# Retention and two expert layers: decay powers by scans, early loads, constants in pieces, noisy logits in two parts

## The chip, the cores and the metric

The program runs on one core of a Trainium2 chip. The metric is the device time of one execution in microseconds (us). The engines are named as the profile names them: PE is TensorE's matmul, PEld its weight load, DVE is VectorE, ACT is ScalarE, POOL is GpSimd, SP is the engine whose queue issues most transfers. An engine takes its instructions in the order in which they stand in its queue; a wait in one holds all behind it.

## What is computed

Two batches of 768 tokens with 8 heads of 64 go through a retention layer, and the 1536 rows of 512 that come out go through two expert layers of 8 experts (512 to 1024 to 512). The part that matters here is the first:

```python
Dmask = np.where(rel >= 0, lam[:, None, None] ** rel[None, :, :], 0.0)
intra = np.einsum('bhic,bhjc->bhij', qb, kb) * Dmask[None]
intra = np.einsum('bhij,bhjd->bhid', intra, vb)
inter = np.einsum('bhid,bhde->bhie', qb * lam_pow[None], kv_state)
out[:, :, sl] = intra + inter
kv_state = lam_block[None, :, None, None] * kv_state + np.einsum('bhsd,bhse->bhde', kb * rev_pow, vb)
```

The second layer's input is chosen by noisy logits: `logits + log1p(exp(x @ w_noise)) * noise`. The two largest of a token name its experts.

## The kernel before, in words

Retention is computed in blocks of 128 tokens instead of the reference's 64, so there are twelve tiles j, six to a batch. For each tile the loop at lines 772 to 819 issues, in this order: the loads of tile j + 2 (`load`, line 152: k, v and, for every second tile, q of two tiles); `scores(j)` (line 610: 16 products of k and q, then the two VectorE products "at" with the decay matrix `dm`); `rows(j - 1)` (line 665: the tile before is turned into rows, its logits are summed on VectorE, its rows are stored to `x1` by SP); `front(j + 1)` (line 604: k and q of the next tile are turned on TensorE; GpSimd makes `kd`, k times the decay factors `dk`, and the four `qd`, q times its powers `pq`); conversions of expert weights (`convert` on ScalarE and `convert_low` on VectorE, lines 101 and 112); `mix(j)` (line 645: the product of `qd` and the state, L651, then of "at" and v, L657, the ScalarE copy `xT`) and, within it, `state(j)` (line 623: the product of `kd` and v, L631, the VectorE sum, and the GpSimd multiply of the state by `dec`, L643); last, loads of expert weights (`fetch`, line 84).

A planner orders each engine's queue by the program's order and by when it expects an instruction to be ready. The author corrects it by hand: `with tc.issue_after(x)` puts each instruction of the block that runs on x's engine behind x in its queue, without a wait, and `behind("name")` does so for the instruction last noted in `turn` under that name.

Before the loop, the powers of lam are made. VectorE doubles a row of powers on 8 partitions (line 187), ScalarE's queue writes it to DRAM (line 189), and two loads read it back as `dm`, each partition a shifted window (line 193). The load of v of tile 0 waits for VectorE (line 190), and k of tile 1 and all after it stand behind the loads of `dm` (line 195). A transpose gives `dk` (line 203), and seven products on 128 partitions give `pq` and `dec` (lines 208 to 216).

Other work is woven into the twelve tiles. GpSimd makes the constants of the expert layers at j = 2 in one run behind `kd` of tile 1 (line 780, `more_constants`). The first expert job takes 288 of the first nine tiles' tokens: the noisy logits of tiles 0 to 5 (`noisy` and `first_marked`, line 811) are made at j = 7, their ranks and one-hot marks at j = 8 (line 806); tiles 6 to 8 follow at j = 9 and 10, and the rows are gathered from `x1` at j = 10 (line 792). Eight parts of the first expert's weights are loaded and converted on the way; the experts then run one after the other, each on 128 to 408 rows, in three products of split numbers (line 842).

Of the kernel before, what the change touches and what calls it, by code (L numbers as in the profile page):

```python
# [8 lines left out]
F32 = mybir.dt.float32  # L9
# [11 lines left out]
P = 128  # L21
# [16 lines left out]
def kernel(ctx: ExitStack, tc: tile.TileContext, q, k, v, lam, g1, gn, noise,  # L38
# [24 lines left out]
    powers = dram.tile([1, H, 2 * P], F32, name="powers")  # L63
# [68 lines left out]
    def wait_for(i, other):  # L132
        tc.add_manual_dep(i.ins, other.ins.name, mybir.DependencyInfo(
            mybir.DependencyClass.Sync, mybir.DependencyReason.DATA), reason="a transfer behind other work")

# [43 lines left out]
    pw = rt.tile([P, 2, ROW], F32, name="xg", bufs=4).rearrange("p a b -> p (a b)")[:H, :2 * P]  # L179
    nc.vector.memset(pw[:, P - 1:P], 1.0)  # L180
    nc.vector.memset(pw[:, P:], 0.0)
    nc.vector.tensor_copy(pw[:, P - 2:P - 1], lamh[:H])
    m = 1
# [17 lines left out]
    dk = consts.tile([P, H, 1], F32, name="dk")  # L201
    ps = bank("yp3", [P, H])
    nc.tensor.transpose(ps, pw[:, :P], ident[:H, :H])
    decays = nc.vector.tensor_copy(dk[:, :, 0], ps).ins
    pq = aw.tile([P, HP, P], F32, name="pq", bufs=1)
    dec = consts.tile([P, HP, 1], F32, name="dec")
# [50 lines left out]
    def more_constants():  # L257
        nc.gpsimd.memset(tri, 1.0)
        nc.gpsimd.affine_select(out=tri, in_=tri, compare_op=OP.is_gt, fill=0.0, base=0,
                                pattern=[[1, P]], channel_multiplier=-1)  # L260
        nc.gpsimd.memset(ones, 1.0)
        iota(slot1, [[1, SLOTS]], 1, 0)
        iota(e_up, [[1, E]], 0, 0)
        iota(e_dn, [[-1, E]], E, 0)
        iota(e_row, [[TS, E]], 0, 0)
        iota(trash, [[P, NT]], TABR, 1)
        iota(tok_t, [[P, NT]], 0, 0)
        iota(tok_p, [[0, 1]], 0, 1)
        iota(steps_p, [[P, 5]], 0, 0)
        past_sizes(past1, FIRST, 4)  # L270
        past_sizes(past2, SECOND, 3)
        for c in range(2):
            nc.gpsimd.tensor_copy(who[:, :, c, 0], tok_p.to_broadcast([P, NT]))
            nc.gpsimd.tensor_scalar(who[:, :, c, 1], tok_t, 1.0 / P, 1.0 + 16 * c, op0=OP.mult, op1=OP.add)
        for a in (aux1, aux2):
            nc.gpsimd.tensor_copy(a[:, :, 0], tok_p.to_broadcast([P, NT]))
            nc.gpsimd.tensor_copy(a[:, :, 1], tok_t)
            nc.gpsimd.memset(a[:, :, 2], 1.0)
        nc.gpsimd.memset(mb1, 0.0)
        nc.gpsimd.memset(mbA, 0.0)  # L280
        nc.gpsimd.memset(mb2, 0.0)
        nc.gpsimd.memset(ent1, 0)
        nc.gpsimd.memset(ent2, 0)
        for c in range(2):
            nc.gpsimd.iota(ent2[:, :, c:c + 1], pattern=[[P, NT], [0, 1]], base=0, channel_multiplier=1)
            nc.gpsimd.iota(ent1[:, :, c, 0:1], pattern=[[P, NT], [0, 1]], base=0, channel_multiplier=1)
            nc.gpsimd.iota(ent1[:, :, c, 1:2], pattern=[[2 * P, NT], [0, 1]], base=c, channel_multiplier=2)
# [296 lines left out]
    def front_k(j):  # L584
# [988 lines left out]
```

## Time and profile before

| | |
|---|---|
| Median of 3 runs | 613.4 us (612.31 to 613.89) |
| Profiled execution | 613.06 us, its span 611.5 us |
| Mean granted TensorE clock | 0.991 |
| PE busy | 588.7 us |
| PEld busy | 555.9 us |
| DVE busy | 373.6 us |
| ACT busy | 279.5 us |
| POOL busy | 183.7 us |

The profile is of one execution. Its span goes from the first to the last instruction, and what is missing to the execution's time lies around it. Busy times are shares of the whole; a stretch has to be looked at by itself to see what limits it. In the timeline, "x8" means eight instructions merged into one line, and the bracket at its end is the idle time before it and what ended that.

### The profile page before, as it was taken

What the parts mean: (1) busy time and instruction counts of PE and PEld (TensorE: products, weight loads), DVE (VectorE), ACT (ScalarE), POOL (GpSimd) and SP (SyncE); (2) the same over time, 40 slices, a digit from 0 to 9 for tenths busy, and PEclk for the clock granted to TensorE, in tenths of its full rate; (3) what the DMA queues carried; (4) which work ended last, traced back from release to release, by engine and by line L of the source; (5) the groups of instructions that cost most, each with busy time, mean ns of one, the idle gap of its engine ahead of it and who ended that gap; (6) DMA issues with size and microseconds to landing.
All of it is one profiled execution on the core that took longest, in us unless ns stands there. A gap on an engine that the chain in (4) does not pass through costs nothing. (4 is left out here: it accounts for less than half of the span.)

```text
span 611.5 us, 11514 instructions
## 1 busy us (share of the span) xinstructions
PE 588.7 (96%) x4261; PEld 555.9 (91%) x4261; DVE 373.6 (61%) x861; ACT 279.5 (46%) x488; POOL 183.7 (30%) x254
## 2 busy tenths in 40 slices
PE   6898899999999999999999999999999999999996
PEld 4787788999999999999999999998889999998995
DVE  4375878967445454363554655465896666666993
ACT  3366442145443353353443534127136466467782
POOL 4953440152405005031050230123165525331203
PEclk9999899999999999999999999999999999999998
DMA  7999620554826437546464440273189967966840
GB/s 173 234 266 237 185 69 31 184 158 144 318 97 217 146 109 259 153 158 209 135 212 138 152 161 1 60 273 114 35 260 346 348 222 226 347 195 201 272 143 34
DMA packets 106081, 110.35 MB, mean 180 GB/s; under 512 B 35895, under 2 KB 81983, under 8 KB 106016
## 3 DMA queue, kind: packets, MB, share of 16 engines
q1 hardware_dynamic: 97936, 83.57, 45.0%
q0 software_dynamic: 8064, 25.95, 12.1%
q8 instruction: 35, 0.57, 0.4%
q14 instruction: 30, 0.25, 0.1%
q10 hardware_dynamic: 16, 0.01, 0.0%
HBM read 92.48 MB, written 18.79 MB: 182 GB/s over the span
## 5 line engine op out<-in xcount | busy, mean ns | idle before, releaser
L115 DVE TENSOR_TENSOR wl<-wst,wh 128x1024 fp32r<-128x1024 f32 x107 | 134.7, 1268 | 53.6 <-ACT wh L109 53.4
L109 ACT CAST wh<-wst 128x1024 fp32r<-128x1024 f32 x107 | 111.1, 1048 | 32.5 <-PE yp L844 25.5
L843 PE MATMUL hp<-x,wh 128*128 128x372 f32 (+9 forms) x352 | 116.5, 331 | 0.8 <-ACTq L1400 0.4
L844 PE MATMUL hp<-x,wh 128*128 128x372 f32 (+9 forms) x352 | 116.0, 330 | 0.0
L845 PE MATMUL hp<-x,wl 128*128 128x372 f32 (+9 forms) x352 | 115.2, 328 | 0.0
L927 ACT ACTIVATE h<-hp 128x372 fp32r<-128x372 f32 (+9 forms) x88 | 41.3, 469 | 156.2 <-PE hp L845 143.1
L843 PE MATMUL yp<-h,wh 128*128 128x372 f32 (+8 forms) x320 | 106.8, 334 | 0.0
L845 PE MATMUL yp<-h,wl 128*128 128x372 f32 (+8 forms) x320 | 106.3, 332 | 0.0
L844 PE MATMUL yp<-h,wh 128*128 128x372 f32 (+8 forms) x320 | 105.5, 330 | 0.0
L928 DVE SCALAR_TENSOR_TENSOR h<-hp,h 128x372 fp32r<-128x372 f32 (+9 forms) x88 | 46.4, 527 | 61.8 <-ACT h L927 61.6
L1050 POOL DMA_INDIRECT x<-y,Rdst x25 | 24.7, 989 | 177.9 <-DVE y L1021 175.9
L843 PEld LDWEIGHTS hp<-x,wh 128*128 128x128 f32 x352 | 66.1, 188 | 2.1 <-ACTq L1400 0.7
L844 PEld LDWEIGHTS hp<-x,wh 128*128 128x128 f32 x352 | 66.2, 188 | 0.5 <-DVE x L1200 0.2
L845 PEld LDWEIGHTS hp<-x,wl 128*128 128x128 f32 x352 | 66.2, 188 | 0.1
L844 PEld LDWEIGHTS yp<-h,wh 128*128 128x128 f32 x320 | 60.3, 188 | 0.3 <-DVE h L928 0.2
L845 PEld LDWEIGHTS yp<-h,wl 128*128 128x128 f32 x320 | 60.3, 188 | 0.2 <-issue 0.2
L843 PEld LDWEIGHTS yp<-h,wh 128*128 128x128 f32 x320 | 60.1, 188 | 0.0
L835 DVE TENSOR_TENSOR x<-tr,x 128x128 fp32r<-128x128 f32 (+11 forms) x68 | 27.4, 435 | 27.5 <-ACT x L834 27.0
L834 ACT CAST x<-tr 128x128 fp32r<-128x128 f32 (+11 forms) x68 | 24.5, 386 | 32.8 <-PE tr L833 32.1
L540 POOL TENSOR_TENSOR xg<-xg 128x512 f32<-128x512 f32 (+1 forms) x16 | 26.3, 1647 | 41.7 <-DMA xg<-x,Tsrc 26.6
L529 POOL DMA_INDIRECT xg<-x,Rsrc x25 | 29.5, 1179 | 18.9 <-DVE slt L499 11.6
L1012 PE MATMUL tr<-iw,yT 128*128 128x136 f32 (+2 forms) x224 | 34.2, 287 | 0.1
(386 smaller groups left out, 1029.2 us busy)
## 6 DMA issues: line engine op xcount, KB each, us to landing
wst<-in_moe_w_dram SPq DMA_DIRECT2D x107, 512.0 KB, 4.9
more<-in_moe_w_dram SPq DMA_DIRECT2D x21, 512.0 KB, 5.6
ldk<-in_k_dram SPq DMA_DIRECT2D x12, 256.0 KB, 5.2
ldv<-in_v_dram SPq DMA_DIRECT2D x12, 256.0 KB, 4.4
x<-xr SPq DMA_DIRECT2D x12, 256.0 KB, 2.8
out_dram<-zero SPq DMA_DIRECT2D x12, 256.0 KB, 5.0
ldq<-in_q_dram SPq DMA_DIRECT2D x5, 512.0 KB, 7.6
ldq<-in_q_dram SPq DMA_DIRECT2D x2, 256.0 KB, 3.7
```

The lines of the kernel that those rows point to most:

```text
L109: tail["cast"] = nc.scalar.copy(hi, st).ins
L115: tail["low"] = nc.vector.tensor_sub(lo, st, hi.bitcast(F32)).ins
L529: i = nc.gpsimd.indirect_dma_start(out=r, out_offset=None, in_=x, in_offset=bass.IndirectOffsetOnAxis(ap=src(s)[:m], axis=0))
L540: tail["both"] = nc.gpsimd.tensor_add(a, a, b).ins
L835: v_ = nc.vector.tensor_sub(lo[:, d, :n], ps[:, :n], hi[:, d, :n].bitcast(F32))
L843: nc.tensor.matmul(ps, a[0], b[0], start=start, stop=False)
L844: nc.tensor.matmul(ps, a[0], b[1], start=False, stop=False)
L845: tail["pe"] = nc.tensor.matmul(ps, a[1], b[0], start=False, stop=stop).ins
L927: tail["act"] = nc.scalar.activation(hh, ps, AF.Relu).ins
L928: tail["dve"] = nc.vector.scalar_tensor_tensor(hl, ps, 0.0, hh.bitcast(F32), op0=OP.max, op1=OP.subtract).ins
L1012: nc.tensor.matmul(ps[:m, i, :], self.yT[:, 2 * b + i, s * r:s * r + m], iw[:, 2 * b + i, gates2], start=True, stop=True)
L1050: i = nc.gpsimd.indirect_dma_start(out=target, out_offset=bass.IndirectOffsetOnAxis(ap=dst, axis=0), in_=y, in_offset=None, bounds_check=t ...
```

## The change

- The row of powers, its store to DRAM and the loads of `dm` go. VectorE makes each head's 128 x 128 decay matrix by a scan along its columns (`dm[:, h, i] = lam * dm[:, h, i - 1] + ident[:, i]`), eight scans. `dk` is the last column of that matrix.
- The powers of q are made by four scans instead of seven products; `dec` is their last column.
- lam is loaded first, to all partitions; v of tile 0 and k, v of tile 1 and q of tile 2 follow without a wait, the gate loads behind them.
- Six products of zeros, which nothing reads, are put ahead of the first transposes on TensorE, and two more between those of k and of q.
- The constants are made in five pieces at j = 0 to 4, each behind the GpSimd multiply of the state.
- Conversions: one at each of j = 2 to 5, instead of one, two, two at j = 3, 4, 5.
- `noisy` is cut in two. For tiles 0 to 5 the first half stands ahead of the scores of j = 7, the rest (`noisy_end`) behind its "at". Ranks and marks stand right behind the scores of j = 8.

```diff
-    lamh = consts.tile([P, 1], F32, name="lamh")
     lamb = consts.tile([P, H], F32, name="lamb")
-    nc.sync.dma_start(lamh[:H], bass.AP(tensor=lam.tensor, offset=lam.offset, ap=[[1, H], [1, 1]]))
+    nc.sync.dma_start(lamb, bass.AP(tensor=lam.tensor, offset=lam.offset, ap=[[0, P], [1, H]]))
     rows_of("k", k, 0)
     load_q(0)
-    nc.sync.dma_start(lamb, bass.AP(tensor=lam.tensor, offset=lam.offset, ap=[[0, P], [1, H]]))
+    written = rows_of("v", v, 0).ins
...
-    while m < P:
-        n = min(m, P - 1 - m)
-        a = P - 1 - m
-        last = nc.vector.tensor_scalar(pw[:, a - n:a], pw[:, P - 1 - n:P - 1], pw[:, a:a + 1], None, op0=OP.mult)
-        m *= 2
-    nc.scalar.dma_start(powers.rearrange("o h m -> (o h) m"), pw)
-    wait_for(rows_of("v", v, 0), last)
-    dm = [aw.tile([P, HP, P], F32, name=f"dm{s}", bufs=1) for s in range(2)]
-    for s in range(2):
-        written = nc.sync.dma_start(dm[s], bass.AP(tensor=powers.tensor, offset=powers.offset + s * 2 * P,
-                                                   ap=[[1, P], [4 * P, HP], [1, P]])).ins
+    def unread(n):
+        ps = bank("yp1", [P, P])
+        for _ in range(n):
+            turn["front"] = nc.tensor.matmul(ps, zero, zero, start=True, stop=True).ins
+
+    turn = {}
+    unread(6)
+
+    dm = aw.tile([P, H, P], F32, name="dm", bufs=1)
+    dk = dm[:, :, P - 1:]
+    for h in range(H):
+        decays = nc.vector.tensor_tensor_scan(dm[:, h, :], lamb[:, h:h + 1].to_broadcast([P, P]), ident, 0.0,
+                                              OP.mult, OP.add).ins
     with tc.issue_after(written):
         rows_of("k", k, 1)
+        rows_of("v", v, 1)
+        load_q(2)
         nc.sync.dma_start(iw[:, :, :E], g1.rearrange("(c p) e -> p c e", p=P))
         nc.sync.dma_start(iw[:, :, E:G], gn.rearrange("(c p) e -> p c e", p=P))
-        rows_of("v", v, 1)
-        load_q(2)
...
-        while m < P:
-            nc.vector.tensor_mul(pq[:, :, m:2 * m], pq[:, :, :m], pq[:, :, m - 1:m].to_broadcast([P, HP, m]))
-            m *= 2
-        nc.vector.tensor_copy(dec, pq[:, :, P - 1:])
+            nc.vector.tensor_copy(lamq[r], lamb[r, s::2])
+        for hp in range(HP):
+            nc.vector.tensor_tensor_scan(pq[:, hp, :], lamq[:, hp:hp + 1].to_broadcast([P, P]), zero, 1.0,
+                                         OP.mult, OP.add)
...
-            kept[j] = nc.gpsimd.tensor_mul(KD[j], qkv["k", j], dk.to_broadcast([P, H, D])).ins
+            i = nc.gpsimd.tensor_mul(KD[j], qkv["k", j], dk.to_broadcast([P, H, D]))
+            turn.setdefault("pool", i.ins)
...
-            turn["at"] = nc.vector.tensor_mul(AT[j, s], ps[s], dm[s][:, :, ::-1]).ins
+            turn["at"] = nc.vector.tensor_mul(AT[j, s], ps[s], dm[:, s::2, :]).ins
...
-        if j == 2:
-            with tc.issue_after(kept[1]):
-                more_constants()
+        if j == T0 + 1:
+            with behind("copied", "lgs"):
+                noisy(s0)
         scores(j)
+        if j == T0 + 2:
+            with behind("scores"):
+                first_ranked(s0, "yp3")
+                marks(ohA, cA, EARLY[0], range(T0))
...
-            for _ in range({3: 1, 4: 2, 5: 2, 8: 1, 10: 1, NT - 1: 1}.get(j, 0)):
+            for _ in range({2: 1, 3: 1, 4: 1, 5: 1, 8: 1, 10: 1, NT - 1: 1}.get(j, 0)):
                 convert()
                 convert_low()
-        if j == T0 + 2:
-            with behind("front", "lgs"):
-                first_ranked(s0, "yp3")
-                marks(ohA, cA, EARLY[0], range(T0))
         if j == T0 + 1:
-            with behind("at", "copied", "lgs"):
-                noisy(s0)
+            with behind("at", "lgs"):
+                noisy_end(s0)
                 first_marked(s0)
         if j:
             mix(j)
+        if j < 5:
+            with behind("pool"):
+                more_constants(j)
```

`noisy` keeps the exponential, the sum with one, the logarithm, the correction's first step and the reciprocal; `noisy_end` has the other four VectorE operations. Piece 0 of the constants holds the masks and number rows, piece 1 and 2 the tables `past1` and `past2`, piece 3 `who` and the auxiliary columns, piece 4 the cleared marks and entries.

## Rows read from the trace of the kernel before

**Rows 1.** A stretch of the expert work: length, busy us (x count) by engine, PEclk, DMA share, GB/s.

```profile
200.00:300.00 100.00, 100.00 (x588) 98.21 (x587) 47.08 (x69) 38.55 (x60) 16.43 (x17) 1.00 0.56 175
```

**Rows 2.** Stretches of tiles 0, 2, 4, 6, 7, 8 and 9, columns as in rows 1.

```profile
9.13:15.15 6.02, 4.89 (x44) 3.91 (x43) 2.13 (x4) 1.17 (x2) 2.83 (x6) 1.00 0.98 223
...
21.45:30.75 9.30, 7.05 (x73) 6.15 (x69) 3.08 (x7) 2.16 (x5) 8.20 (x25) 0.83 1.14 301
...
37.17:42.83 5.66, 5.49 (x73) 4.97 (x69) 5.34 (x9) 4.22 (x8) 4.66 (x5) 1.00 0.86 219
...
48.67:55.35 6.68, 4.76 (x62) 4.02 (x60) 4.82 (x7) 3.73 (x7) 1.73 (x3) 1.00 0.93 254
55.35:61.66 6.31, 6.23 (x78) 5.61 (x76) 3.13 (x9) 4.02 (x10) 3.19 (x4) 1.00 0.89 227
61.66:71.11 9.45, 6.71 (x79) 6.16 (x75) 8.37 (x24) 3.23 (x6) 3.63 (x5) 0.87 0.86 236
71.11:77.94 6.83, 6.75 (x78) 6.02 (x77) 4.52 (x17) 3.83 (x9) 2.08 (x3) 0.94 0.27 77
```

**Rows 3.** Timeline of the first 16 us: start, us, engine, line, operation, tiles.

```profile
2.34 0.14 DVE L182 COPY xg<-lamh 8x1 f32<-8x1 f32 x1 [0.93 <-DMA lamh<-in_lam_dram]
...
6.33 0.43 DVE L561 COPY qp<-ldq 128x512 f32<-128x512 f32 x1 [1.40 <-DMA ldq<-in_q_dram]
6.67 0.34 DVE L211 COPY pq<-lamb 64x4 f32<-64x4 f32 x2
6.76 0.92 SPq L193 DMA_DIRECT2D dm<-powers  x2
...
9.13 1.83 PE L617 MATMUL tr<-qT,kT 64*128 64x128 f32 x16
...
10.99 1.29 DVE L621 TENSOR_TENSOR at<-tr,dm 128x512 f32<-128x512 f32 x2 [0.81 <-PE tr L617]
...
12.33 1.09 PE L657 MATMUL yp<-at,ldv 128*64 128x128 f32 x14 [0.17 <-DVE at L621]
...
12.94 1.04 POOL L593 TENSOR_TENSOR kd<-ldk,dk 128x512 f32<-128x512 f32 x1 [3.19 <-DMA ldk<-in_k_dram]
...
15.15 1.16 PE L617 MATMUL tr<-qT,kT 64*128 64x128 f32 x16
```

**Rows 4.** Timeline of GpSimd's constants, first and last, and what follows them.

```profile
14.61 0.21 POOL L258 MEMSET tri<- 128x128 bf16 x1
...
22.23 0.49 SPq L91 DMA_DIRECT2D wst<-in_moe_w_dram  x1
...
23.80 0.29 POOL L285 IOTA ent<- 128x12 int32 x2
...
25.06 2.76 POOL L579 TENSOR_TENSOR qd<-qT,pq 128x256 f32<-128x256 f32 x4
...
25.83 0.71 PE L651 MATMUL yp<-qd,st 128*128 128x128 f32 x4 [1.60 <-POOL qd L579]
```

**Rows 5.** Timeline of tile 6's conversions and the rows behind them.

```profile
48.28 2.00 ACT L109 CAST wh<-wst 128x1024 fp32r<-128x1024 f32 x2
...
50.18 0.59 ACT L661 COPY xT<-yp 128x512 f32<-128x512 f32 x1
...
50.82 1.25 PE L672 MATMUL yp<-iw,xT 128*128 128x144 f32 x8 [0.99 <-ACT xT L661]
```

**Rows 6.** Timeline of tile 8: the noisy logits' run and the ranks.

```profile
64.39 0.96 DVE L704 TENSOR_TENSOR ln<-ln,nz 128x48 f32<-128x48 f32 x1
...
67.41 0.18 PE L319 MATMUL yp<-mbA,tri 128*128 128x7 bf16 x1 [2.75 <-DVE mbA L714]
```

**Rows 7.** Groups of VectorE, first 100 us: line, operation, count, busy us, mean ns.

```profile
L214 DVE TENSOR_TENSOR pq<-pq 128x256 f32<-128x256 f32 x1 | 0.4, 424 | 0.0
...
L214 DVE TENSOR_TENSOR pq<-pq 128x128 f32<-128x128 f32 x1 | 0.3, 291 | 0.0
```

**Rows 8.** Transfers issued in the first 100 us: count, KB each, median us to landing.

```profile
wst<-in_moe_w_dram SPq DMA_DIRECT2D x8, 512.0 KB, 4.7
```

More of the change, by code (lines that the diff above doesn't have):

```diff
@@ L62 @@
     tab2 = dram.tile([TABR + TS, 4], I32, name="tab2")
-    powers = dram.tile([1, H, 2 * P], F32, name="powers")
     def bank(tag, shape, dt=F32):
@@ L130 @@
     qkv = {}
-    def wait_for(i, other):
-        tc.add_manual_dep(i.ins, other.ins.name, mybir.DependencyInfo(
-            mybir.DependencyClass.Sync, mybir.DependencyReason.DATA), reason="a transfer behind other work")
     def rows_of(n, src, j):
@@ L176 @@
     nc.gpsimd.tensor_copy(iw[:, 1:, G:G + P], ident[:, None, :].to_broadcast([P, DC - 1, P]))
[L179 to L183, printed above, removed]
[L184 to L194 removed]
+    def unread(n):
[9 more added lines that the diff above has]
+                                              OP.mult, OP.add).ins
     with tc.issue_after(written):
         rows_of("k", k, 1)
+        rows_of("v", v, 1)
+        load_q(2)
         nc.sync.dma_start(iw[:, :, :E], g1.rearrange("(c p) e -> p c e", p=P))
         nc.sync.dma_start(iw[:, :, E:G], gn.rearrange("(c p) e -> p c e", p=P))
[L199 to L204 removed]
     pq = aw.tile([P, HP, P], F32, name="pq", bufs=1)
[L206 removed]
+    dec = pq[:, :, P - 1:]
+    lamq = consts.tile([P, HP], F32, name="lamq")
     def powers_of_q():
@@ L255, in past_sizes @@
                     nc.gpsimd.memset(c, 0.0 if m else 1.0)
[L257 to L287, printed above, removed]
@@ new lines, in more_constants @@
+    def more_constants(piece):
+        if piece == 0:
+            nc.gpsimd.memset(tri, 1.0)
+            nc.gpsimd.affine_select(out=tri, in_=tri, compare_op=OP.is_gt, fill=0.0, base=0,
+                                    pattern=[[1, P]], channel_multiplier=-1)
+            nc.gpsimd.memset(ones, 1.0)
+            iota(slot1, [[1, SLOTS]], 1, 0)
+            iota(e_up, [[1, E]], 0, 0)
+            iota(e_dn, [[-1, E]], E, 0)
+            iota(e_row, [[TS, E]], 0, 0)
+            iota(trash, [[P, NT]], TABR, 1)
+            iota(tok_t, [[P, NT]], 0, 0)
+            iota(tok_p, [[0, 1]], 0, 1)
+            iota(steps_p, [[P, 5]], 0, 0)
+        elif piece == 1:
+            past_sizes(past1, FIRST, 4)
+        elif piece == 2:
+            past_sizes(past2, SECOND, 3)
+        elif piece == 3:
+            for c in range(2):
+                nc.gpsimd.tensor_copy(who[:, :, c, 0], tok_p.to_broadcast([P, NT]))
+                nc.gpsimd.tensor_scalar(who[:, :, c, 1], tok_t, 1.0 / P, 1.0 + 16 * c, op0=OP.mult, op1=OP.add)
+            for a in (aux1, aux2):
+                nc.gpsimd.tensor_copy(a[:, :, 0], tok_p.to_broadcast([P, NT]))
+                nc.gpsimd.tensor_copy(a[:, :, 1], tok_t)
+                nc.gpsimd.memset(a[:, :, 2], 1.0)
+        else:
+            nc.gpsimd.memset(mb1, 0.0)
+            nc.gpsimd.memset(mbA, 0.0)
+            nc.gpsimd.memset(mb2, 0.0)
+            nc.gpsimd.memset(ent1, 0)
+            nc.gpsimd.memset(ent2, 0)
+            for c in range(2):
+                nc.gpsimd.iota(ent2[:, :, c:c + 1], pattern=[[P, NT], [0, 1]], base=0, channel_multiplier=1)
+                nc.gpsimd.iota(ent1[:, :, c, 0:1], pattern=[[P, NT], [0, 1]], base=0, channel_multiplier=1)
+                nc.gpsimd.iota(ent1[:, :, c, 1:2], pattern=[[2 * P, NT], [0, 1]], base=c, channel_multiplier=2)
@@ L547 @@
     QT, KT, QD, KD, AT, XT = {}, {}, {}, {}, {}, {}
-    kept, stored = {}, {}
+    stored = {}
     def pair(t, hp):
@@ L600, in behind @@
         return stack
-    turn = {}
     def front(j):
-        with behind("rows" if j > 1 else "state"):
+        with behind("rows" if j > 1 else "state" if j else "front"):
             front_k(j)
+        if not j:
+            with behind("front"):
+                unread(2)
+        with behind("rows" if j > 1 else "state" if j else "front"):
             if j % 2 == 0:
@@ L642, in state @@
             if c + 1 < NC - 1:
-                nc.gpsimd.tensor_mul(st[c % 2], new, dec.to_broadcast([P, HP, P]))
+                turn["pool"] = nc.gpsimd.tensor_mul(st[c % 2], new, dec.to_broadcast([P, HP, P])).ins
     def mix(j):
@@ L688 @@
     entered1 = []
+    noised = {}
     mbA, cA, doneA = consts.tile([P, TA + 1, 1], BF16, name="mbA"), small("cA", [P, TA]), small("doneA", [P, 1])
     def noisy(sl):
-        n = sl.stop - sl.start
         ex, up, ln, cr = (small(x, full)[:, sl] for x in ("ex", "up", "ln", "cr"))
@@ L701, in noisy, with noisy_end @@
         nc.vector.reciprocal(up, up)
+        noised[sl.start] = up, ln, cr
+    def noisy_end(sl):
+        up, ln, cr = noised[sl.start]
         nc.vector.tensor_mul(cr, cr, up)
@@ L796 @@
                 noisy(s1)
+                noisy_end(s1)
                 turn["marked"] = first_marked(s1)
@@ L1226 @@
         noisy(tB)
+        noisy_end(tB)
     choices1()
```

2 lines of the change are left out of this document (removed).

## The prediction

> **What bounds the kernel now.** I read a stretch from the middle of the expert work first: TensorE is busy 100.00 us in 100 there [rows 1]. After the first stage nothing but TensorE's own work counts, and a change that leaves the experts alone can only move the moment at which they begin. The edit lies wholly ahead of that moment, in the twelve tiles of retention. So the second view is a table of stretches, each from the first score product of one tile to that of the next [rows 2]. The reader is to compare two columns there: the length of a stretch and what TensorE was busy in it. Tile 4's stretch is 5.66 us with 5.49 busy and tile 7's 6.31 with 6.23: these are full (an odd tile also turns two tiles of q). Four are not: tile 0 (6.02, 4.89 busy), tile 2 (9.30), tile 6 (6.68, 4.76 busy) and tile 8 (9.45). [...]
>
> Third, the timeline of each of the four says what ended the idle time.
> - **Tile 0** [rows 3]. VectorE waits for lam until 2.34 and makes the powers; the transfers that read them back from DRAM leave SP's queue at 6.76, and k of tile 1 only behind them. GpSimd gets it at 12.94, after 3.19 us idle. The first scores take 1.83 us where tile 1's take 1.16, and the products with v end at 12.33 + 1.09 = 13.42.
> - **Tile 2** [rows 4]. GpSimd makes all its constants in one run, from 14.61 to 23.80 + 0.29 = 24.09, with one state multiply of kd's shape inside. Behind it come kd and, at 25.06, four qd products of 2.76 in all. TensorE idles 1.60 us for the first of them.
> - **Tile 6** [rows 5]. Two conversions of weights in a row on ScalarE, 2.00, hold the copy xT, for which TensorE waits 0.99.
> - **Tile 8** [rows 6]. The noisy logits of six tiles stand in one run on VectorE ahead of "at". One operation of it, 48 columns wide, takes 0.96. TensorE waits 2.75 us for the marks at the end of the run, and all that is behind the ranks in its queue waits too.
>
> **The change part by part.** The sum is made against the profiled execution, 613.06 us (span 611.5; 1.56 lies around it). The median of the runs shown is 613.4, so 0.3 is added at the end.
>
> *Powers and loads (tile 0).* Removed: a chain of seven VectorE operations on 8 partitions, a transpose, the write of the powers, the two reads of dm and two waits on SP's queue. Added on VectorE: eight scans for dm and four for the powers of q, these in place of seven products and a copy. No scan is in the trace. The nearest row is a two-input operation of the same 128 columns, 0.291. It can hardly cost less than a small copy, 0.34 / 2 [rows 3]; the dearest small operation is the 0.96 of tile 8 [rows 6, 7]. I take 0.29. Lam now goes to 128 partitions instead of 8; I take 2.9 for its arrival instead of 2.34. Eight scans end at 2.9 + 2.3 = 5.2. The copy of q's second half waited for its transfer until 6.33 anyway [rows 3]: that load hides the eight, and if it came earlier they would show. Then VectorE has 0.43 for the copy, 0.34 for two small ones, 4 x 0.29, and twice 256 columns for the first state, 2 x 0.424 [rows 7], to 9.1. kd's factor dk comes half a microsecond later than now. Against that, eight products of zeros on TensorE should bring the clock up sooner, which takes 0.67 off the scores and about as much off the transposes and the state before them. I put the end of the scores at 9.5, "at" (1.29) at 10.8, the products with v at 11.4 instead of 13.42. k of tile 1 leaves SP some 4 us sooner and is there by then. On SP's queue v, k, v and q of the next tiles now pass the two gate loads; these are wanted by the rows of tile 0, three microseconds behind its scores. Term: -2.0, bounds -3.0 and 0.
>
> [...]
>
> *Constants in five pieces (tile 2).* The run of 9.5 us less one state multiply, 8.4, becomes five pieces, 1.7 on average and 2.5 for a long one by my estimate, one behind each tile's state multiply. GpSimd's own work per tile is kd 1.04, a state multiply of the same shape and half of four qd products, 3.5 in all; with a piece 5.2 to 6.0, against a stretch of 5.7 to 6.3. So GpSimd is nearly full in tiles 0 to 4, and what is late next is whatever stands behind a piece. The qd products are wanted three microseconds into the stretch; a piece ahead of them would cost up to its length. At best tile 2 falls from 9.30 to tile 4's 5.66, -3.6. I take -3.0, bounds -3.6 and -1.1 (a long piece ahead of qd).
>
> *Conversions (tiles 2 to 6).* One at each of tiles 2 to 5 instead of one, two, two from tile 3. The eighth falls to the experts, where the last part of the second matrix is wanted six steps later; nothing waits. Tile 6 had 6.68 - 4.76 = 1.9 idle: -1.5, bounds -1.9 and 0. The price is at tile 2, where ScalarE now converts the first part. That part leaves SP at 22.23 now [rows 4] and takes 4.7 [rows 8]. Two microseconds earlier it lands at 24.9; 2.00 / 2 for the conversion and 0.59 for xT behind it [rows 5] make 26.5. Tile 3's stretch would begin at 19.4 + 5.7 = 25.1 and wants xT behind its scores, 1.16 into it, at 26.3. With a little on top I put +0.5, bounds 0 and +5.0 (the part takes twice the 4.7).
>
> *Noisy logits divided, ranks earlier (tile 8).* The first half of the chain goes ahead of tile 7's scores, the rest behind its "at", in a stretch in which VectorE is busy 3.13 of 6.31 [rows 2]. The ranks then stand behind tile 8's scores with their marks done. Tile 8 becomes tile 4's 5.66 plus 0.5 of rank products: -3.3. With no idle time the clock stays up into tile 9 (0.94 there now), -0.3 of its 6.83. I take -3.4, bounds -3.7 and -2.0.
>
> *Nothing, each hidden:* strided reads of dm and pq instead of dk and dec (as many elements; GpSimd's 3.5 us per tile covers them where no piece stands); the noisy logits of tiles 6 to 11, the same operations in the same order.
>
> Sum: -2.0 - 3.0 - 1.5 + 0.5 - 3.4 = -9.4. 613.06 - 9.4 + 0.3 = 604.0.
>
> **The rivals.**
> 1. *A new wait on ScalarE.* The conversion at tile 2 waits as long as the bound says, 5.0 instead of 0.5, with xT and all of tile 2's rows queued behind it: 608.5. For it: ScalarE takes its work in order, and the load stands behind the store of tile 0. Against: the row has 4.7 for such loads.
> 2. *The transfers set the pace.* Before tile 9 starts, q, k and v (9.4 MB by their shapes), eight weight parts (4.2) and eight stored tiles (2.1) must have moved, 15.7 MB, in 69 us now. At tile 8's 236 GB/s [rows 2] they need 66.5, and tile 9 would start 2.6 us sooner: 610.8. Against: tile 2 moved 301 GB/s, and the last wait for k that is longer than 0.2 us is tile 1's [rows 3]. If GpSimd's pieces are ordered badly too, nothing is left that can be measured.
> 3. *The scans are slow, and the kernel slower.* The copy of q's half, the powers of q, the first state and "at" are queued on VectorE behind them. At a price P the products with v end at 2.9 + 0.43 + 0.34 + 0.85 + 1.29 + 1.1 + 12 P = 6.9 + 12 P, where that is later than 11.4. At 0.96 that is 18.4, five later than now, and with 7.4 gained in the other terms the time is 611. From P = 1.16 on nothing is gained; from 1.3 on it is slower by over 0.3%; at 1.5 it is 617. The near rows speak against it.
>
> That the zeros do not bring the clock up is inside the first term: 0.7 to 1.0 of it is then lost.
>
> **How the numbers follow.** Forecast 0.62, first rival 0.20, second 0.13, third 0.05. Low end: all terms at their good ends, -12.2, give 601.2, and half of the spread of the runs shown takes it to 600.5. High end: the first rival and one microsecond of the other bad ends, 609.5. A measurement of this kernel tells about 0.3%, 1.8 us, from no change. Faster: the forecast, the first rival and a third of the second, 0.87. Same: the rest of the second, 0.08. Slower: the third, 0.05.
>
> **What would show it.** Right: tile 1's scores near 13 instead of 15.15; no wait of TensorE for qd in tile 2, whose stretch is near 6; tile 8's stretch near 6 at clock 1.00; tile 9 starting near 61.7 instead of 71.11, and everything from there on as long as now. Wrong: a wait for wst ahead of xT in tile 2, a scan over 0.5 us, waits for k or v, or an expert stream that grew by what the start gained.

## The result and the profile after

The changed kernel takes 602.77 us (median of 4 runs, 602.37 to 605.96) against 612.86 for the kernel before on the same chip (4 runs, 611.16 to 613.89): a ratio of 0.985, 95% interval 0.982 to 0.988. The profiled execution took 602.82 us, with a span of 601.2 and a mean granted clock of 0.998. PE is busy 586.7 us (588.7 before), VectorE 375.1 (373.6), ScalarE 279.7 (279.5), GpSimd 183.6 (183.7). TensorE's idle time in the span goes from 22.8 to 14.5 us, which is most of the gain. Its busy time falls by 2.0 although the products of zeros, 4.0 us, are new in it: less of the work runs at a granted clock below 1.00 (tile 2: 7.05 us busy at 0.83 before [rows 2], 5.08 at 1.00 after).

The table has the start of each tile's score products and, last, of the experts' first product, in the two profiled executions. The last column is what that stretch added to the difference.

| tile | before | after | after minus before | added since the row above |
|---|---|---|---|---|
| 0 | 9.13 | 9.41 | +0.28 | +0.28 |
| 1 | 15.15 | 14.64 | -0.51 | -0.79 |
| 2 | 21.46 | 20.95 | -0.51 | 0.00 |
| 3 | 30.75 | 26.03 | -4.72 | **-4.21** |
| 4 | 37.18 | 32.35 | -4.83 | -0.11 |
| 5 | 42.83 | 37.72 | -5.11 | -0.28 |
| 6 | 48.67 | 43.57 | -5.10 | +0.01 |
| 7 | 55.36 | 48.72 | -6.64 | **-1.54** |
| 8 | 61.66 | 55.03 | -6.63 | +0.01 |
| 9 | 71.11 | 60.29 | -10.82 | **-4.19** |
| 10 | 77.94 | 66.71 | -11.23 | -0.41 |
| 11 | 85.97 | 74.75 | -11.22 | +0.01 |
| experts | 93.47 | 82.79 | -10.68 | +0.54 |

From the experts' first product to the end it is 518.0 us before and 518.4 after, so nearly all of the 10.7 reached the end. In the fourteen profiles of this case that part lasts 517.1 to 519.1, though no edit touches its products; differences of less than that can't be put down to an edit. The start varies too: in the seven profiles whose front is as in the changed kernel, tile 0's scores start between 9.21 and 10.09, and where tile 0 is otherwise untouched tile 1's start between 14.43 and 15.34. So the -0.51 at tile 1 is one execution's figure.

The view of stretches of the changed kernel, tiles 0, 2, 4, 6, 7, 8 and 9 and 100 us of the expert work (length, busy us and count of PE, PEld, DVE, ACT and POOL, granted clock, DMA share, GB/s), answers to [rows 2] and [rows 1]:

```profile
9.41:14.64 5.23, 4.11 (x47) 3.17 (x43) 2.28 (x5) 1.25 (x3) 5.23 (x16) 1.00 1.24 208
...
20.95:26.03 5.08, 5.08 (x72) 4.77 (x68) 3.69 (x8) 2.86 (x6) 4.80 (x17) 1.00 1.11 326
...
32.35:37.72 5.37, 5.37 (x72) 4.97 (x69) 5.06 (x9) 3.27 (x7) 4.35 (x5) 1.00 1.15 295
...
43.57:48.72 5.15, 4.76 (x62) 4.02 (x61) 3.97 (x9) 3.27 (x8) 3.01 (x3) 1.00 1.11 286
48.72:55.03 6.31, 6.23 (x78) 5.62 (x77) 4.03 (x15) 3.83 (x8) 3.22 (x4) 1.00 0.84 242
55.03:60.29 5.26, 5.26 (x79) 4.95 (x75) 4.87 (x15) 2.86 (x6) 3.66 (x5) 1.00 0.96 241
60.29:66.71 6.42, 6.34 (x80) 5.62 (x76) 5.29 (x18) 4.13 (x10) 2.49 (x3) 1.00 0.98 260
189.30:289.30 100.00, 100.00 (x589) 98.21 (x588) 46.98 (x68) 38.72 (x62) 16.44 (x17) 1.00 0.57 177
```

Tiles 2 and 8 went from 9.30 and 9.45 to 5.08 and 5.26, and TensorE is busy for the whole of both, at clock 1.00. Tile 4, which the prediction took for full at 5.66, is 5.37 now. Of the tiles shown only 0 and 6 still have more than 0.1 us idle; of the others, tiles 1, 10 and 11 have (0.75, 0.58 and 1.42 in the same view). The experts' row is as before.

The timeline of the changed kernel (start, us, engine, line, operation, and the idle time before it with what ended it), answering to [rows 3] to [rows 6]:

```profile
3.84 2.63 DVE L184 TENSOR_TENSOR_SCAN dm<-lamb,iw 128x128 f32<-128x128 f32 x8 [2.49 <-DMA lamb<-in_lam_dram]
...
6.56 1.06 POOL L584 TENSOR_TENSOR kd<-ldk,dm 128x512 f32<-128x512 f32 x1 [3.55 <-DVE dm L184]
6.81 1.09 DVE L552 COPY qp<-ldq 128x512 f32<-128x512 f32 x1 [0.34 <-DMA ldq<-in_q_dram]
...
8.19 1.37 DVE L201 TENSOR_TENSOR_SCAN pq<-lamq,zero 128x128 f32<-128x128 f32 x4
...
9.41 1.16 PE L611 MATMUL tr<-qT,kT 64*128 64x128 f32 x16
...
11.95 1.09 PE L651 MATMUL yp<-at,ldv 128*64 128x128 f32 x14 [0.16 <-DVE at L615]
...
17.17 1.34 SPq L90 DMA_DIRECT2D wst<-in_moe_w_dram  x1
...
19.74 2.78 POOL L570 TENSOR_TENSOR qd<-qT,pq 128x256 f32<-128x256 f32 x4 [4.34 <-ACT qT L565]
...
23.56 1.06 PE L645 MATMUL yp<-qd,st 128*128 128x128 f32 x8
...
24.30 1.05 ACT L108 CAST wh<-wst 128x1024 fp32r<-128x1024 f32 x1
...
25.69 0.59 ACT L655 COPY xT<-yp 128x512 f32<-128x512 f32 x1 [0.34 <-PE yp L651]
...
44.18 2.40 POOL L570 TENSOR_TENSOR qd<-qT,pq 128x256 f32<-128x256 f32 x2
44.27 1.72 DVE L114 TENSOR_TENSOR wl<-wst,wh 128x1024 fp32r<-128x1024 f32 x1 [2.14 <-ACT wh L108]
...
52.30 0.21 DVE L703 TENSOR_TENSOR ln<-ln,nz 128x48 f32<-128x48 f32 x1
...
53.34 0.17 DVE L713 TENSOR_SCALAR mbA<-cA 128x6 bf16<-128x6 f32 x1
...
56.12 0.18 PE L310 MATMUL yp<-mbA,tri 128*128 128x7 bf16 x1
...
76.40 0.93 POOL L520 DMA_INDIRECT xg<-x,Asrc  x1 [0.31 <-issue]
...
80.44 0.38 PE L1199 MATMUL tr<-iw,xg 96*128 96x96 f32 x2 [1.04 <-DMA xg<-x,Asrc]
```

Where TensorE waited 1.60 for qd, GpSimd has made tile 2's four products by 22.52, a microsecond before they are wanted (23.56). Where it waited 2.75 for the marks, they are done 2.6 us ahead of the ranks (53.51 against 56.12). ScalarE's conversion in tile 2 holds nothing up: xT behind it waits for TensorE. The wait for gathered rows in tile 11 has grown from 0.28 to 1.04. The kernel before, for comparison:

```profile
87.62 0.92 POOL L529 DMA_INDIRECT xg<-x,Asrc  x1 [0.31 <-issue]
...
90.91 0.39 PE L1196 MATMUL tr<-iw,xg 96*128 96x96 f32 x2 [0.28 <-DMA xg<-x,Asrc]
```

TensorE wants the second gathered piece 3.0 us after its issue in both kernels; it came after 3.29 before and after 4.04 now. In the runs below it came after 3.2 to 5.4. Why is open.

### The profile page after: what moved, and what is told of

Same layout as the page of the kernel before. It is cut to its first block, busy times and chain, and to the rows that moved or that the text cites. A ratio compares the mean times of both kernels' runs of the same rounds, so it can differ in the third digit from the quotient of the medians.

```text
span 601.2 us, 11534 instructions
## 1 busy us (share of the span) xinstructions
PE 586.7 (98%) x4276; PEld 555.1 (92%) x4276; DVE 375.1 (62%) x854; ACT 279.7 (47%) x488; POOL 183.6 (31%) x254
## 5 line engine op out<-in xcount | busy, mean ns | idle before, releaser
L531 POOL TENSOR_TENSOR xg<-xg 128x512 f32<-128x512 f32 (+1 forms) x16 | 23.5, 1473 | 44.1 <-DMA xg<-x,Tsrc 27.8
```

## The experiments

Times are medians, and ratios are to the kernel before on the same chip. Diffs are against the changed kernel unless said otherwise.

**Constants in one run again, behind kd of tile 1, all else changed.**

```diff
+        if j == 2:
+            with tc.issue_after(kept[1]):
+                for piece in range(5):
+                    more_constants(piece)
...
-        if j < 5:
-            with behind("pool"):
-                more_constants(j)
```

> The changed kernel, with GpSimd's constants again in one run at tile 2, behind kd of tile 1. Theory (each part gives back TensorE's idle time of one tile, and the parts add): tile 2's stretch goes from 5.08 back to about 9.3, its qd wait of TensorE returns, the time is some 4.2 us longer than the changed kernel's (about 607). Rival (the stalls went because loads begin sooner, so undoing one part alone costs little): tile 2's stretch stays under 6.5 and the time within 1.5 us of the changed kernel's.

Measured: 610.75 us, ratio 0.997 (0.9956 to 0.9985), span 609.3. That is 8.1 of span more than the changed kernel, about twice what the run of constants cost before, and not in tile 2 (5.09). kd of tile 1 is ready sooner now, and so the run stood at 10.42 to 19.5, ahead of tile 1's qd. Its timeline:

```profile
10.42 0.20 POOL L245 MEMSET tri<- 128x128 bf16 x1
...
17.98 0.72 POOL L570 TENSOR_TENSOR qd<-qT,pq 128x256 f32<-128x256 f32 x1
...
18.76 1.22 PE L646 MATMUL yp<-qd,st 128*128 128x128 f32 x4 [4.91 <-POOL qd L570]
...
21.02 2.08 PE L612 MATMUL tr<-qT,kT 64*128 64x128 f32 x16
```

TensorE waits 4.91 for qd, and the scores behind it take 2.08 instead of 1.16. Tile 0 grew from 5.23 to 11.38 and tile 1 from 6.31 to 8.26. The expectation (tile 2 back at 9.3) was wrong about the place and the size; that TensorE waits for qd behind the run was right.

**One run again, but behind tile 0's state multiply, where the first piece stands.**

```diff
-        if j < 5:
+        if j == 0:
             with behind("pool"):
-                more_constants(j)
+                for piece in range(5):
+                    more_constants(piece)
```

> The changed kernel with all constants in one run, but behind the state multiply of tile 0 instead of ahead of it. By the changed kernel's rows the run then goes from 12.7 to about 21.2, kd of tile 2 to 22.2, and the four qd that TensorE wants from 23.45 on start at 22.2. Theory (what counts is whether the run stands ahead of something that TensorE wants soon, not whether it is cut): tile 2's stretch grows by 0.5 to 1.0, the time by as much. Rival (it must be cut): 3 us or more longer.

Measured: 603.30 us, ratio 0.9839 (0.982 to 0.9858), an interval that holds the changed kernel's 0.985. The run stands at 12.71 to 22.1 with kd of tile 2 inside, and tile 2's qd follows at 22.15:

```profile
20.86:26.43 5.57, 5.35 (x72) 4.85 (x69) 3.97 (x8) 2.87 (x6) 5.57 (x13) 1.00 1.11 320
```

Tile 1 is untouched (6.31) and tile 2 loses 0.49. So the cut into pieces is not what gained four microseconds; the place was: behind tile 1's qd and early enough for tile 2's. The profiled execution is the slowest of the four (604.68); 1.6 of the 1.9 by which its span is longer stand in tile 11, where the gathered rows are waited for 2.43.

**The pieces alone, in the kernel before.**

```diff
-        if j == 2:
-            with tc.issue_after(kept[1]):
-                more_constants()
...
+        if j < 5:
+            with behind("pool"):
+                more_constants(j)
```

> The kernel before with the constants in five pieces and nothing else of the change. Theory: tile 2's stretch falls from 9.30 to 5.1 to 5.7, TensorE's wait for qd goes; 3.6 to 4.2 us faster than before. Rival (a piece or the planner's new order puts the wait elsewhere): under 2 us faster.

Measured: 610.21 us, ratio 0.9954 (0.9938 to 0.9971), a gain of 3.0. The stretches of tiles 0 and 2, one microsecond of tile 0, and TensorE's first wait in tile 0:

```profile
9.24:16.66 7.42, 5.68 (x45) 4.70 (x43) 2.30 (x5) 1.17 (x2) 4.13 (x8) 0.77 0.93 216
...
22.96:28.05 5.09, 5.09 (x72) 4.78 (x68) 3.02 (x7) 1.92 (x5) 4.77 (x20) 1.00 1.09 310
...
14.00:15.00 1.00, 1.00 (x7) 0.67 (x5) 0.00 (x0) 0.49 (x1) 1.00 (x3) 0.50 0.65 177
...
11.81 0.43 PE L663 MATMUL yp<-at,ldv 128*64 128x128 f32 x2 [1.23 <-DVE at L627]
```

Tile 2 falls to 5.09 as in the changed kernel, -4.2, by the pieces alone. Tile 0, with the old front, is 7.42 long, 1.4 more than in the profile of before: there "at" waited for dm from DRAM and TensorE for "at" (1.23 and 0.51 idle), and behind that the granted clock reads 0.50 (14.00 to 15.00). In the profile of before [rows 2] it reads 1.00 in tile 0, behind the same front. The ten executions of this kernel spread accordingly: mean granted clocks of 0.996 to 0.999 go with spans of 606.3 to 608.8, and 0.989 to 0.993 with 608.4 to 610.5. So the old front seems to have this loss in some executions and not in others. Tile 6 is 5.83 here, 0.86 less than before, with its conversions as they were; the section on the prediction comes back to that.

**The noisy logits in one piece behind tile 7's "at", with the ranks behind the front of tile 9.**

```diff
-        if j == T0 + 1:
-            with behind("copied", "lgs"):
-                noisy(s0)
         scores(j)
-        if j == T0 + 2:
-            with behind("scores"):
-                first_ranked(s0, "yp3")
-                marks(ohA, cA, EARLY[0], range(T0))
...
         if j == T0 + 1:
-            with behind("at", "lgs"):
+            with behind("at", "copied", "lgs"):
+                noisy(s0)
                 noisy_end(s0)
```

(with the ranks and marks put back behind "front" and "lgs")

> The changed kernel, with the noisy logits of tiles 0 to 5 again in one piece behind tile 7's at, and ranks and marks behind the front of tile 9. Theory: tile 8's stretch goes from 5.26 back to about 9, the clock falls in it, tile 9 starts at the lower clock; the time is 4.2 to 4.6 us longer. Rival (one conversion less at tiles 4 and 5 and GpSimd's lighter load already free VectorE for it): under 1.5 us longer.

Measured: 607.45 us, ratio 0.9917 (0.9892 to 0.9942), span 605.9, 4.7 more than the changed kernel's. Tile 8:

```profile
55.70:65.47 9.77, 6.99 (x80) 6.39 (x76) 8.40 (x24) 2.94 (x6) 3.66 (x5) 0.83 0.71 195
```

The old stretch is back, with its clock (0.83; 0.87 in [rows 2]). The expectation held, a tenth past its range (4.2 to 4.6).

**The chain divided, the ranks late as before.**

```diff
-        if j == T0 + 2:
-            with behind("scores"):
-                first_ranked(s0, "yp3")
-                marks(ohA, cA, EARLY[0], range(T0))
...
+        if j == T0 + 2:
+            with behind("front", "lgs"):
+                first_ranked(s0, "yp3")
+                marks(ohA, cA, EARLY[0], range(T0))
```

> The changed kernel with ranks and marks of tiles 0 to 5 again behind the front of tile 9, the noisy logits still in two parts. Theory (the division alone made the marks ready in time): tile 8's stretch stays within 0.5 of 5.26, the time within 0.5 us. Rival (the earlier ranks were needed, since at of tile 8 and the rank products share VectorE and TensorE): 1.5 us or more longer.

Measured: 602.29 us, ratio 0.9838 (0.9816 to 0.986), tile 8 5.36 against 5.26. The division with its first half ahead of tile 7's scores does it; where the ranks stand is worth a tenth, which the times don't show. The kernel before has one more row that bears on this:

```profile
61.10 0.19 DVE L697 TENSOR_SCALAR up<-ex 128x48 f32<-128x48 f32 x1 [2.56 <-ACT ex L696]
```

The whole chain began only here, at the end of tile 7's stretch, after VectorE had waited 2.56 for ScalarE's exponential, and it then ran beside GpSimd's qd, kd and state multiply. In the changed kernel the exponential is made in tile 6. No run moved the chain ahead of tile 7's scores undivided, so whether it had to be cut, or only to begin earlier, is open.

**Conversions as before.**

```diff
-            for _ in range({2: 1, 3: 1, 4: 1, 5: 1, 8: 1, 10: 1, NT - 1: 1}.get(j, 0)):
+            for _ in range({3: 1, 4: 2, 5: 2, 8: 1, 10: 1, NT - 1: 1}.get(j, 0)):
```

> The changed kernel, with one, two and two conversions at tiles 3, 4 and 5 again instead of one at each of 2 to 5. Theory: tile 6's stretch goes from 5.15 back to about 6.7 and nothing else moves: 1.5 us longer. Rival (tile 6 became short because VectorE and GpSimd no longer meet there): within 0.5 us.

Measured: 605.47 us, ratio 0.9886 (0.9852 to 0.9921). Tile 4's stretch is 5.67; those of tiles 5 and 6:

```profile
38.52:45.18 6.66, 5.74 (x63) 5.07 (x61) 5.20 (x9) 3.77 (x8) 6.48 (x24) 1.00 1.07 286
45.18:51.47 6.29, 4.76 (x62) 4.02 (x60) 4.77 (x9) 4.03 (x8) 1.34 (x2) 1.00 0.73 217
```

And the timeline at tile 6's start:

```profile
44.84 2.00 ACT L108 CAST wh<-wst 128x1024 fp32r<-128x1024 f32 x2
...
47.38 1.25 PE L666 MATMUL yp<-iw,xT 128*128 128x144 f32 x8 [1.04 <-ACT xT L655]
```

The wait of [rows 5] is back (1.04, 0.99 there). The loss stands in three tiles, 0.30 + 0.81 + 1.14 = 2.25, where one was expected to carry it: for tile 5 VectorE's half of the two conversions, wl, takes 3.20 beside GpSimd's state multiply, and TensorE waits 0.92 for the sum of the state that is queued on VectorE behind it. The span is 3.4 longer; the rest of that is 0.51 at tile 0's start, within what executions differ by, and 0.7 in the experts, which was not followed up.

**No products of zeros.**

```diff
-    unread(6)
+    unread(0)
...
-                unread(2)
+                unread(0)
```

> The changed kernel without the eight products of zeros on TensorE. Theory: the transposes and scores of tile 0 run at the lower clock until about 11 us, as before; the scores of tile 0 take 1.83 instead of 1.16 and those of tile 1 start 0.7 to 1.2 us later; the whole is longer by as much. Rival (the zeros stand in front of the transposes and only delay them; the loads set the start): tile 1's scores start within 0.2 us of 14.64, the time the same.

Left out are only products that nothing reads. Measured: 603.59 us, ratio 0.9853 (0.9827 to 0.988). Its timeline in tile 0:

```profile
10.08 2.08 PE L611 MATMUL tr<-qT,kT 64*128 64x128 f32 x16
...
12.94 2.57 PE L651 MATMUL yp<-at,ldv 128*64 128x128 f32 x16 [0.78 <-DVE at L615]
```

And the stretch of tile 0, from its scores to tile 1's:

```profile
10.08:17.28 7.20, 6.42 (x44) 5.28 (x42) 2.13 (x4) 1.17 (x2) 5.27 (x16) 1.00 1.06 176
```

TensorE's products in tile 0 are faster with the products of zeros ahead of them: without them the scores take 2.08 (1.16 in the changed kernel) and the 16 products with v 2.57 (0.43 + 1.09 there), and tile 1 starts 2.64 us later, more than twice what was expected. That they run at a lower clock, as the theory has it, is not shown: the granted clock reads 1.00 in tile 0 in the kernel before [rows 2], in the changed one and here. Yet the span is only 0.7 longer (601.9). Tile 6 gave back 0.49 (4.66 instead of 5.15) and tile 11 0.45 (7.59 instead of 8.04); the experts start at 84.46, 1.67 later, and their part is 1.0 shorter, which is within its spread. Why tile 6 gives back is in the last section; in tile 11 the gathered rows came 3.24 after their issue, as in the kernel before. The time can't be told from the changed kernel's (602.77, and 603.16 when it was run again), so no gain of the zeros in the whole is shown.

**The powers through DRAM again, all else changed** (core of the edit).

```diff
-    for h in range(H):
-        decays = nc.vector.tensor_tensor_scan(dm[:, h, :], lamb[:, h:h + 1].to_broadcast([P, P]), ident, 0.0,
-                                              OP.mult, OP.add).ins
...
+    nc.scalar.dma_start(powers.rearrange("o h m -> (o h) m"), pw)
+    wait_for(rows_of("v", v, 0), last)
...
+        written = nc.sync.dma_start(dm[s], bass.AP(tensor=powers.tensor, offset=powers.offset + s * 2 * P,
+                                                   ap=[[1, P], [4 * P, HP], [1, P]])).ins
     with tc.issue_after(written):
         rows_of("k", k, 1)
```

> The changed kernel with the powers made as before (VectorE's row of powers, the store, the two loads of dm, the two waits on SP's queue, the seven products for q), zeros, pieces and all else as changed. Theory (the front gained only half a microsecond, since a contended copy of q's half and later loads took the rest): tile 1's scores start at 14.6 to 15.6, the time is 0 to 1 us longer than the changed kernel's. Rival (the front's loads are what the later tiles live on): 2 us or more longer, with waits for k or weights in tiles 2 to 8.

Measured: 605.34 us, ratio 0.9879 (0.9863 to 0.9896), span 602.7. Tile 0's stretch:

```profile
8.38:15.92 7.54, 5.15 (x45) 4.08 (x43) 2.67 (x6) 1.17 (x2) 3.36 (x5) 0.83 0.93 217
```

And its timeline behind the scores:

```profile
10.71 0.69 DVE L637 TENSOR_TENSOR at<-tr,dm 128x512 f32<-128x512 f32 x1 [1.00 <-DMA dm<-powers]
...
11.46 0.43 PE L673 MATMUL yp<-at,ldv 128*64 128x128 f32 x2 [1.92 <-DVE at L637]
...
12.56 1.04 POOL L606 TENSOR_TENSOR kd<-ldk,dk 128x512 f32<-128x512 f32 x1 [6.52 <-DMA ldk<-in_k_dram]
```

The scores start a microsecond sooner than in the changed kernel (8.38), but "at" waits 1.00 for dm, TensorE 1.92 for "at", and kd of tile 1 until 12.56 for a load that is queued behind dm. The granted clock of the stretch is 0.83, and tile 1 starts at 15.92, 1.28 later. By the spans the new front is worth 1.5, by the ratios 1.8, by the medians 2.6 (605.34 - 602.77); the profiled execution is the fastest of the four. That is more than the theory's 0 to 1. It stands in the front and not, as the rival had it, in waits for k or weights in tiles 2 to 8, which together are 0.3 shorter than in the changed kernel.

**The changed kernel again, and kd of tile 0 held until VectorE's copy of q is done.**

```diff
+            tc.add_manual_dep(decayed(0).ins, i.ins.name, mybir.DependencyInfo(
+                mybir.DependencyClass.Sync, mybir.DependencyReason.DATA), reason="behind the copy of q")
...
-            i = nc.gpsimd.tensor_mul(KD[j], qkv["k", j], dk.to_broadcast([P, H, D]))
-            turn.setdefault("pool", i.ins)
+            if j:
+                decayed(j)
```

> The changed kernel as it is, beside the next three on the same chip. 602.3 to 603.5.

> The changed kernel, with kd of tile 0 on GpSimd waiting for VectorE's copy of q's second half, which took 1.09 us beside kd and 0.43 in the kernel before. Theory (the two share a way to the buffer): the copy takes 0.43 to 0.5, tile 0's scores start 0.4 to 0.7 earlier against the load of q, tile 1's by 0.2 to 0.6; in the total no more than 0.6, under what a run can tell. Rival (the copy is slow because loads land in the buffer at the same time, or because of the scans before it): the copy stays at 0.9 or more.

Measured: 603.16 us for the changed kernel, ratio 0.9844 (0.982 to 0.9869), and 602.67, ratio 0.9828 (0.9805 to 0.985), with kd held. The timeline of the latter:

```profile
6.84 0.43 DVE L552 COPY qp<-ldq 128x512 f32<-128x512 f32 x1 [0.37 <-DMA ldq<-in_q_dram]
...
7.36 1.08 POOL L590 TENSOR_TENSOR kd<-ldk,dm 128x512 f32<-128x512 f32 x1 [4.35 <-DVE qp L552]
7.55 2.11 DVE L201 TENSOR_TENSOR_SCAN pq<-lamq,zero 128x128 f32<-128x128 f32 x4
```

The copy falls from 1.03 to 0.43, and now the scans of q's powers stand beside kd and take 2.11 instead of 1.37. So the copy did as the theory had it, though what the two engines share no run shows. But tile 1's scores start at 14.76 instead of 14.82, not 0.2 to 0.6 earlier, and the times can't be told apart.

**lam from ScalarE's queue, so that it doesn't stand ahead of k in SP's.**

```diff
-    nc.sync.dma_start(lamb, bass.AP(tensor=lam.tensor, offset=lam.offset, ap=[[0, P], [1, H]]))
+    nc.scalar.dma_start(lamb, bass.AP(tensor=lam.tensor, offset=lam.offset, ap=[[0, P], [1, H]]))
```

> The changed kernel, with lam loaded from ScalarE's queue beside k's load on SP's instead of ahead of it. Theory (lam's load ahead of k and q delays both by 0.4): k is there by 4.7 instead of 5.1, q's halves 0.4 sooner, tile 1's scores near 14.2. Rival (TensorE's zeros or the scans set the start): tile 1's scores stay at 14.4 to 14.7. In the total at most 0.5.

Measured: 603.62 us, ratio 0.9845 (0.9821 to 0.9868). Two lines of its timeline:

```profile
4.43 2.63 DVE L184 TENSOR_TENSOR_SCAN dm<-lamb,iw 128x128 f32<-128x128 f32 x8 [3.08 <-DMA lamb<-in_lam_dram]
...
5.58 1.09 PE L579 MATMUL hp<-iw,ldk 128*128 128x128 f32 x4 [1.46 <-DMA ldk<-in_k_dram]
```

All came later, not sooner: lam at 4.43 instead of 3.82 and k at 5.58 instead of 5.08, though both were issued at 0.94. Tile 1's scores start at 15.59. The next kernel has the same edit and the same delays (4.38 and 5.53), so this is no chance of one execution. Neither the theory nor the rival said that, and why is open.

**Both of these, and the second gathered piece turned behind the last rows of retention instead of ahead of them.**

```diff
-        with tc.issue_after(turn["state"] if s < EARLY[1] - 1 else tail["rows"]):
+        with tc.issue_after(turn["state"] if s < EARLY[1] - 2 else tail["rows"]):
```

> Both edits of the front together, and the second of the three gathered pieces of rows turned behind the last rows of retention instead of ahead of them, where TensorE waited 1.04 us for its gather. Theory: 0.4 to 0.8 from the front, 0.5 from the gather, 601.5 to 602.2. Rival (the gather's third piece ends as late anyway): no gain from the second part.

Measured: 603.31 us, ratio 0.9843 (0.9818 to 0.9867). No gain, where 601.5 to 602.2 was expected: tile 1 starts at 15.14, the experts at 83.12. The wait for the second piece has gone, but the third is waited for 0.55, as the rival had it, and tile 11 is 8.36 long instead of 8.04. No version tried beats the changed kernel by more than the spread.

## Why the prediction was right, and which of its terms were not

The forecast's 604.0 had -9.4 in it; the profiled executions differ by 10.24 (613.06 - 602.82), the medians by 10.1. What bounds the kernel was read rightly: the experts' stream kept its length to 0.4 us, so what tiles 0 to 11 saved is what the kernel saved. The terms did worse than their sum. They missed by up to 1.5 in both directions (+1.5 in tile 0; -1.2 each in tiles 2 and 8; -0.3 and -0.5 by the conversions and their price; +0.9 not foreseen), and what is left of that is 0.8. That the sum came so near is in part luck.

- **Tile 0, -2.0.** Mis-sized: in the profiles -0.51 stands at tile 1's start, which was to be near 13 and is 14.64. Three steps failed. lam arrived at 3.84, not 2.9. A scan took 0.33 (2.63 / 8), not 0.29. And the copy of q's half, put at 0.43, took 1.09, because kd on GpSimd was let go by the last scan just before it (kd from 6.56, the copy from 6.81; with kd held back the copy takes 0.43). With the measured values the third rival's formula gives 3.84 + 0.34 (wait for q) + 1.09 + 0.33 + 0.85 + 1.29 + 1.09 + 4.00 = 12.83; the products with v ended at 13.04, not 11.4. The part is nevertheless worth 1.5 to 2.6 when it alone is undone, since the old front then waits for dm (1.00) and loses clock (0.83; 0.77 with the pieces alone), which it did not in the one profile of before (1.00 [rows 2]). That is near the -2.0, but by luck: the term was worked out from steps of which three failed, against a front that had not waited for dm in its profile. That the zeros would bring the clock up was the author's estimate; the runs show the durations, 1.83 for the scores before, 1.16 now and 2.08 without the zeros, with the granted clock of tile 0 at 1.00 each time.
- **The price of a scan.** It was put at that of a two-input operation of the same 128 columns. By the trace one scan of 128 columns lasts 402 ns on average, beside 291 for 128 columns of a two-input operation and 424 for 256 [rows 7]. In a row the scans follow each other every 0.33, and that is what the sum needed. Why a scan lasts longer than an operation of its width is open.
- **Tile 2, -3.0.** It gave -4.21, past the good bound of -3.6. The bound came from tile 4's 5.66, taken for full; tile 4 itself held idle time and is 5.37 now. A full even stretch is 5.08. That GpSimd would be nearly full was right (4.80 of 5.08). The reason was only half right: not the division but the place decides, as the two kernels with one run show (+8.1 and +0.5).
- **Conversions, -1.5.** -1.54 at tile 6 and -0.28 at tile 4; undone, 2.25. The size is right, a little small. The wait that it was read from, 0.99 for xT behind ScalarE's two conversions, is not the one that ends last in tile 6. In the kernel before:

```profile
49.37 3.25 DVE L115 TENSOR_TENSOR wl<-wst,wh 128x1024 fp32r<-128x1024 f32 x2 [2.40 <-ACT wh L109]
...
53.28 0.43 PE L657 MATMUL yp<-at,ldv 128*64 128x128 f32 x2 [0.77 <-DVE at L621]
```

"at" is queued on VectorE behind its halves of the conversions, wl, and TensorE waits for it again, 0.77 and 0.16, behind the products that had waited for xT. The stretch follows wl: 3.25 became 1.72, a fall of 1.53, and the stretch fell by 1.54. With two conversions in tile 6 it is 6.69, 6.29 and 5.83 long (before, conversions as before, pieces alone) at 3.25, 2.81 and 2.40 of wl. So part of the gain is not the moved conversion but how long GpSimd held VectorE up: in the kernel before, kd began at 49.35 beside the first wl, which took 2.12, and the second took 1.21; with the pieces alone both took 1.23. No run took away ScalarE's half or VectorE's alone; this is read from the rows.
- **ScalarE's wait for the weights, +0.5.** It is 0, so the first rival fell with it: the first part left SP at 17.17, not two microseconds ahead of 22.23, and the conversion began at 24.30 with nothing waiting. The shorter queue on SP moved the load five microseconds, not two.
- **Tile 8, -3.4.** -4.19, and -0.41 in tile 9 where the clock stays at 1.00 (0.94 in [rows 2]): -4.60, past the bound of -3.7, for the same reason as in tile 2. The two experiments on this part put the cause on the noisy logits and not on the ranks; whether the cut or the earlier start did it is open.
- **Not foreseen:** +0.54 in tile 11, where the gathered rows are waited for 1.04 (0.28 before), and +0.4 in the experts, which is within their spread.

Against the second rival, tile 2 moved 326 GB/s, and tile 9 started at 60.29, not 2.6 us ahead of 71.11. Against the third, 0.33 is far from the 1.16 at which nothing would be gained.

## What to carry to other kernels

When TensorE is full behind some point, sum what each stretch ahead of it holds in idle time, and do not take the length of a stretch that looks full as the floor of its kind: tile 4's 5.66, 5.49 of it busy, stood for a floor here, and two tiles of its kind came to 5.08 and 5.26. When a wait is to be shortened, look for the one that ends last in its stretch, on the other engines' queues too. A long run of small work on an engine costs by what stands behind it in its queue; moving it whole to a place with slack was worth as much here, to half a microsecond, as cutting it up, and the same run at the wrong place lost eight microseconds. Ahead of costing an instruction at its duration elsewhere, look whether its new neighbour on VectorE or GpSimd will run at the same moment: the copy of q's half lasted 0.43 here, and 1.09 beside kd.

## What the runs showed of the hardware that was not expected

**VectorE beside GpSimd.** In tile 6 of the changed kernel, qd on GpSimd starts at 44.18 and wl on VectorE at 44.27 (timeline above). The durations of these two qd products, by the view of the tile qd in that stretch (shortest, median, longest ns; first and last start):

```profile
L570 POOL TENSOR_TENSOR qd<-qT,pq x2: 726/1217/1708, 44.2 to 44.9; 128x256 f32<-128x256 f32 x2
```

The first takes 0.73 and wl, which starts beside it, 1.72; the second starts at 44.9 beside wl and takes 1.71. In the kernel with the old front qd was over as wl began, and wl took 1.23:

```profile
44.67 1.42 POOL L592 TENSOR_TENSOR qd<-qT,pq 128x256 f32<-128x256 f32 x2 [1.69 <-ACT qT L587]
...
46.06 1.23 DVE L115 TENSOR_TENSOR wl<-wst,wh 128x1024 fp32r<-128x1024 f32 x1 [3.04 <-ACT wh L109]
```

Each time the one that began first ran its usual time and the other lasted about as long as the rest of that and its own: 44.18 + 0.73 + 1.23 = 46.14, and wl ended at 45.99, 0.15 sooner. The copy of q's half fits this too (beside kd, 6.56 + 1.06 + 0.43 = 8.05; it ended at 7.90), and so does the operation of 0.96 in [rows 6], 0.21 in the changed kernel: in the kernel before GpSimd's state multiply had begun ahead of it,

```profile
64.25 1.04 POOL L643 TENSOR_TENSOR st<-st,dec 128x512 f32<-128x512 f32 x1
```

and 64.25 + 1.04 + 0.21 = 65.50, where it ended at 65.35. Not every pair does so: in tile 0 of the changed kernel VectorE's two "at" take 1.29 from 10.61 on, beside two qd (1.41 from 10.37 on), as they did in the kernel before with GpSimd idle [rows 3]. What sets the pairs apart no run shows. The prediction costed kd and the copy each as if it ran alone.

**Why the front's gain stops at tile 6.** In the eleven profiled kernels with one conversion there, the changed one and ten of the experiments, tile 6's stretch less the time of wl in it is 3.43 or 3.44: 5.15 - 1.72, 5.25 - 1.82 and 5.02 - 1.59 where wl met qd, 4.66 - 1.23 (no zeros, old front) where qd was over, and 4.71 - 1.27 (lam on ScalarE's queue) where wl began first and qd took the delay (2.40 for the two). With two conversions, in the other three, it is 3.43 to 3.48. A front some tenths later or earlier shifts the two engines against each other, and half a microsecond is lost or regained. This is read from all of those rows; no run moved qd of tile 6 by itself, so whether that half microsecond can be kept is open.

**A slow product at a granted clock of 1.00.** Without the products of zeros, the scores of tile 0 took 2.08 instead of 1.16, while the column of the granted clock reads 1.00 in both. With the old front the same column fell to 0.50 behind 1.74 of idle time in two waits (the pieces alone). The column therefore doesn't show every loss of speed; the duration of a known group of products does. That duration also shows that the speed rises at different moments with the same front: the state's 16 products just ahead of tile 0's scores took 0.69 in the changed kernel and 1.12 in the run with the noisy logits whole. Without the zeros they took 1.12 too, at 1.00 in the column (0 to 10).
